# Attention, a product layer and a routed layer in one kernel: items of chunk 2 leave chunk 0's last two steps, and three hand-written orders are changed

## The chip, the cores and the metric

The kernel runs on one core of one Trainium2 chip. The metric is the device time of one execution in microseconds (us), as the median of several runs. A core has five engines that each run their own queue of instructions in order: TensorE (PE, with PEld for its weight loads), VectorE (DVE), ScalarE (ACT), GpSimd (POOL) and SyncE (SP, which issues most DMAs here). They meet at semaphores. Matrix products are written to PSUM, which is used here in named banks, everything else lives in SBUF.

## The reference

Three layers follow each other over N = 2304 tokens of 512 features (4 batches of 576 tokens, 8 heads of 64):

```python
scores = where(mask, q @ k^T / sqrt(64) + bias, -1e9)      # causal, window 128
x = softmax(scores) @ v                                     # (2304, 512)
x = ((x @ w_a) * (x @ w_b)) @ w_out                         # d_ff = 1536
logits = x @ w_gate + modality_bias[modality_id]            # 8 experts
e = argmax(logits); gate = softmax(logits)[e]
out = gate * (relu(x @ w1[e]) @ w2[e])                      # d_ff = 1024, one expert per token
```

All of it is float32. Products that need the full precision are made from two parts of each operand, a high part that is rounded for TensorE's fast format and the rest, as three matmuls (high times high, high times rest, rest times high). In the arrays the weights `w_a`, `w_b` and `w_out` are 64-bit floats; the kernel turns them into 32-bit ones with integer operations on VectorE (`f64_ops`, L422 and L426, three operations for each piece).

## The kernel before

**Tiles and chunks.** The 18 tiles of 128 tokens are cut into seven chunks of `CH = [3,2,2,3,3,3,2]` tiles. For each chunk the middle layer runs in 12 steps j, one for each 128 of the 1536 inner features. A step multiplies the chunk's x by the column pieces j of `w_a` and `w_b` (`mm_ab`, L513, 12 matmuls each, into banks `ab0` and `ab1`), copies the first product to SBUF (`asb`, ACT), multiplies the second by it (`gf`, DVE), splits `gf` into high part and rest (`g`: ACT, then DVE) and adds the product of the step before with its piece of `w_out` into the bank of each token tile (`mm_out`, L526 in chunk 0, L530 later).

**Attention as items.** Attention is cut into 72 items, one for each chunk, pair of heads and token tile; items 0 to 11 are chunk 0's, 12 to 19 chunk 1's, 20 to 27 chunk 2's. While a chunk's middle layer runs, its steps also carry the items of the chunk that comes next. The table `goal` says up to which item the scores are made by the end of each step. An item passes through three steps. In the first its scores are made (`ps_s`, PE; L254 for chunk 1's items, L258 for later ones), masked and reduced (DVE L266, L272) and exponentiated (ACT L282). In the next step the sums are inverted (DVE L288, L290), the exponentials scaled (ACT L301), transposed (`ps_p`, PE L310), copied as `pc` (ACT L323, DVE L324) and masked into `pt` by two selects (POOL L326, L328). In the third `a_pv` multiplies `pt` by V (`ps_o`, PE L378), and `pv_out` copies it out of its bank (`u`, ACT L387), moves one part across partitions (`z`, a DMA) and adds the parts into `xf` (POOL L392, and L393 once `z` has landed). When a chunk's items are done, `x_split` makes `xr` from `xf` (ACT L412, DVE L413), which the next chunk's L513 multiplies. Each pair of heads of chunk 2 or later is prepared once: `kk` (ACT L173, DVE L177), `qq` (ACT L183, DVE L188) and `vv` (ACT L197, DVE L201). `new_preps` starts them two steps ahead by `goal`; their DVE half is put off to the next step (`late_rests`).

**What chunk 0 does besides.** In chunk 0 the steps (`step0`) also convert weights. VectorE makes 32-bit floats of the next step's pair of pieces (`f64f`, jobs `w`) and of a piece of `w_out` (`f64o`, `wo_jobs`); ScalarE makes the high part of the pair (`wab`, L454, the "high parts"), VectorE the rest (L457). `mm_out` of chunk 0 uses `f64o` straight. In the last step (j = 11) two pieces of `w_out` are converted. In chunk 1 each step splits one piece of `w_out` into high part and rest (`wo_split`: ACT L497, DVE L498).

**Routing.** When a chunk's middle layer is done its token tiles are copied out (L634), and the router of the third layer runs for them during the next chunk. For chunks 0 and 1 that is `route` and `route_fin`: transposes (L542), then logits (L550) and arithmetic on VectorE (L557 to L576), then the rank of each token within its expert, two short matmuls (L585, L586) and five small VectorE operations (L587 to L592). One token tile takes three steps; the state in `tr` says where it stands.

**What sets the order.** The order of PE, ACT and DVE is the order in which the code is written, by hand. That of POOL and SP is left to a scheduler. `step0` writes out the order of VectorE's jobs as a string of letters: `w` an operation on the output weights, `l` the same for the last piece, `i` an inversion, `a` an operation on the pair's weights.

## Time and profile before

| what | value |
|---|---|
| median of 3 runs | 818.93 us (818.31 to 819.97) |
| the profiled execution, whole | 818.71 us |
| its span, first to last instruction | 816.9 us |
| chunk 0's steps | about 34 to 136 us |
| chunk 1's steps | about 136 to 204 us |
| chunk 2's steps | about 204 to 273 us |

The page gives PE 97% of the span as busy, DVE 67%, ACT 56% and POOL 29%. Matmuls are pipelined in the records, so what a reader looks for on PE is not its busy share but the places where a row of its timeline has an idle time in brackets, with the engine, tile and line that ended it. Between rows the distance from start to start is the time that a piece of work takes from the engine. The mean granted clock of TensorE is 0.995 of full speed over the span, and 1.00 in the three stretches of the table.

### The profile page before, as it was taken

To read this page: it belongs to the slowest core of one execution; us is meant where nothing else is said; L and a number is where in the kernel's file an instruction comes from. 1 tells how busy PE (TensorE), PEld (TensorE's weight loads), DVE (VectorE), ACT (ScalarE), POOL (GpSimd) and SP (SyncE) were. 2 spreads that over 40 slices of the span, in tenths; PEclk is the share of its full clock that TensorE was granted. 3 is DMA by queue.
4 is the path that set the end of the run, shared out by engine and by line. 5 is a ranking of instruction groups with operands and counts; after the bars stand their busy time and mean duration, and the time that the engine had idled before them with its cause. 6 is when DMAs were issued, how large, how long until landed. Compare 5 with 4: busy or idle time off the path is not lost.

```text
span 816.9 us, 14394 instructions
## 1 busy us (share of the span) xinstructions
PE 796.3 (97%) x4686; PEld 720.6 (88%) x4686; DVE 547.7 (67%) x1581; ACT 461.3 (56%) x1171; POOL 236.6 (29%) x365
## 2 busy tenths in 40 slices
PE   9999989999999999999999999999999999999994
PEld 7877767898899999999999999999988898989893
DVE  7899997777666766768776776468676544447410
ACT  6865447877678766666667643223436454457420
POOL 5332361443243333333333331120233030303101
PEclk9999999999999999999999999999999999999997
DMA  8977546777656875554556544566539464629201
GB/s 242 367 252 263 172 134 178 216 227 232 176 161 175 208 192 160 143 170 132 164 145 155 137 131 127 147 193 211 191 102 318 162 207 117 221 93 325 103 14 41
DMA packets 78629, 145.13 MB, mean 178 GB/s; under 512 B 14095, under 2 KB 41903, under 8 KB 78544
## 3 DMA queue, kind: packets, MB, share of 16 engines
q1 hardware_dynamic: 74992, 134.39, 54.7%
q0 software_dynamic: 3552, 9.73, 3.2%
q8 instruction: 39, 0.64, 0.3%
q14 instruction: 46, 0.38, 0.2%
HBM read 118.16 MB, written 22.12 MB: 172 GB/s over the span
## 4 chain that ended last, share of the span: by engine, by line
PE 62%; issue 14%; DVE 11%; ACT 7%; POOL 2%; DMA 2%; SPq 0%; POOLq 0%; ACTq 0%; DVEq 0%
PE ps_ab L513 29%; PE acc L530 12%; PE ps_h L1316 5%; PE ps_y L1299 4%; PE ps_o L378 2%; PE ps_s L258 2%; DVE f64f L426 2%; PE acc L526 2%; ACT p L282 2%; PE ps_p L310 1%; POOL out L1306 1%; PE ps_s L254 1%; DVE f64o L426 1%; POOL xg L940 1%; DMA wr<-in_moe_w 1%
## 5 line engine op out<-in xcount | busy, mean ns | idle before, releaser
L513 PE MATMUL ps_ab<-xr,wab 128*128 128x384 f32 (+1 forms) x2016 | 325.3, 316 | 0.9 <-DVE xr L413 0.7
L513 PEld LDWEIGHTS ps_ab<-xr,wab 128*128 128x128 f32 x2016 | 306.7, 188 | 11.8 <-issue 2.6
L530 PE MATMUL acc<-wo,g 128*128 128x512 f32 x540 | 135.4, 393 | 0.0
L326 POOL TENSOR_SCALAR_AFFINE_SELECT pt<-pc 128x512 fp32r<-128x512 f32 (+1 forms) x72 | 48.2, 669 | 257.1 <-DVE pc L324 232.6
L530 PEld LDWEIGHTS acc<-wo,g 128*128 128x128 f32 x540 | 96.9, 188 | 16.9
L1316 PE MATMUL ps_h<-xT,w1s 128*128 128x384 f32 x576 | 104.4, 337 | 0.0
L1299 PE MATMUL ps_y<-w2s,h 128*128 128x512 f32 x432 | 103.2, 393 | 0.0
L1316 PEld LDWEIGHTS ps_h<-xT,w1s 128*128 128x128 f32 x576 | 99.9, 188 | 0.9
L1299 PEld LDWEIGHTS ps_y<-w2s,h 128*128 128x128 f32 x432 | 79.8, 188 | 15.6
L282 ACT ACTIVATE p<-p,mx 128x128 f32<-128x128 f32 x144 | 56.8, 396 | 35.3 <-DVE mx L272 35.2
L613 DVE CUSTOM_DVE_ANT_0 junk<-x,wgt 128x512 f32<-128x512 f32 x88 | 62.3, 708 | 2.0
L1306 POOL DMA_INDIRECT out<-y,idx x18 | 20.4, 1134 | 133.1 <-ACT y L1305 131.9
L387 ACT COPY u<-ps_o 64x384 f32<-64x384 f32 x120 | 56.9, 474 | 2.0 <-PE ps_o L378 0.6
L1148 ACT CAST g<-gf 128x384 fp32r<-128x384 f32 (+1 forms) x60 | 28.2, 471 | 50.7 <-DVE gf L1146 50.3
L301 ACT ACTIVATE p<-p,mx 128x128 f32<-128x128 f32 x120 | 41.8, 395 | 26.7 <-DVE mx L290 26.5
L1149 DVE TENSOR_TENSOR g<-gf,g 128x384 fp32r<-128x384 f32 (+1 forms) x60 | 30.3, 505 | 38.1 <-ACT g L1148 38.1
L1146 DVE TENSOR_TENSOR gf<-ps_ab,asb 128x384 f32<-128x384 f32 (+1 forms) x60 | 30.1, 502 | 32.2 <-PE ps_ab L513 25.0
L900 DVE TENSOR_TENSOR w2s<-wr,w2s 128x1024 fp32r<-128x1024 f32 x24 | 29.2, 1224 | 32.9 <-ACT w2s L899 32.8
L900 DVE TENSOR_TENSOR w1s<-wr,w1s 128x1024 fp32r<-128x1024 f32 x28 | 34.3, 1224 | 20.9 <-ACT w1s L899 20.7
L328 POOL TENSOR_SCALAR_AFFINE_SELECT pt<-pc 128x512 fp32r<-128x512 f32 (+1 forms) x72 | 48.2, 669 | 0.0
L1319 ACT ACTIVATE h<-ps_h 128x384 fp32r<-128x384 f32 x48 | 23.6, 491 | 40.0 <-PE ps_h L1316 40.0
L392 POOL TENSOR_TENSOR xf<-u 128x128 f32<-128x128 f32 x60 | 33.5, 558 | 43.3 <-ACT u L387 43.3
(218 smaller groups left out, 1200.5 us busy)
## 6 DMA issues: line engine op xcount, KB each, us to landing
wo<-wo_d SPq DMA_DIRECT2D x60, 512.0 KB, 3.9
wr<-in_moe_w SPq DMA_DIRECT2D x56, 512.0 KB, 4.4
wgt<-in_wgt SPq DMA_DIRECT2D x32, 256.0 KB, 3.6
wraw<-in_moe_w_a SPq DMA_DIRECT2D x12, 512.0 KB, 5.7
wraw<-in_moe_w_b SPq DMA_DIRECT2D x12, 512.0 KB, 6.2
wor<-in_moe_w_out SPq DMA_DIRECT2D x12, 512.0 KB, 3.8
wo_d<-wo SPq DMA_DIRECT2D x12, 512.0 KB, 3.5
kr<-in_k SPq DMA_DIRECT2D x24, 256.0 KB, 4.1
```

The costliest lines, as they stand in the source:

```text
L282: nc.scalar.activation(out=it.p[:, h, :], in_=it.p[:, h, :], func=AF.Exp, bias=it.mx[:, 2 + h:3 + h], scale=-1.0, accum_out=it.mx[:, 4 + h ...
L301: nc.scalar.activation(out=it.p[:, h, :], in_=it.p[:, h, :], func=AF.Copy, scale=it.mx[:, 6 + h:7 + h])
L326: nc.gpsimd.affine_select(out=it.pt[:, :, 0], in_=pc, pattern=pat + [[-1, P]], base=0, channel_multiplier=1, compare_op=ALU.is_gt, fill=0.0)
L328: mark["pt"] = nc.gpsimd.affine_select(out=it.pt[:, :, 1], in_=pc, pattern=pat + [[1, P]], base=0, channel_multiplier=-1, compare_op=ALU.i ...
L387: nc.scalar.copy(out=u[o:o + 64], in_=it.po[o:o + 64, 1 - h:4 - h])
L392: nc.gpsimd.tensor_tensor(out=xf, in0=u[:, 0], in1=u[:, 2], op=ALU.add)
L513: nc.tensor.matmul(ps[:, :n], lhsT=w[:, m, r, kk * P:(kk + 1) * P], rhs=xr[:, s, kk, :n], start=(idx == 0), stop=(idx == len(terms) - 1))
L530: nc.tensor.matmul(acc[c, t], lhsT=g[:, r, t * P:(t + 1) * P], rhs=w[:, s, :], start=(j == 0 and idx == 0), stop=(j == NJ - 1 and idx == 2))
L613: nc.vector.tensor_tensor_reduce(out=junk, in0=x2[:, 0:DM], in1=wgt[e % len(wgt)], scale=1.0, scalar=0.0, op0=ALU.mult, op1=ALU.add, accum ...
L900: nc.vector.tensor_tensor(out=dst[:, 1], in0=srcw, in1=dst[:, 0], op=ALU.subtract)
L1299: nc.tensor.matmul(pss[t], lhsT=h[:, r, f, t * P:(t + 1) * P], rhs=W2[f // 2][:, s_, f % 2, :], start=(f == 0 and i == 0), stop=(f == 7 an ...
L1316: nc.tensor.matmul(ps, lhsT=W1[f // 2][:, r, kk, (f % 2) * P:(f % 2 + 1) * P], rhs=xT[:, s_, kk, :], start=(kk == 0 and i == 0), stop=(kk ...
```

## The change

There are five edits.

- `goal`: in chunk 0 the steps 10 and 11 make no scores any more; before, they made those of items 20 and 21, chunk 2's first two. Chunk 1's twelve steps take 11 items in place of 9. The preparations of the pairs move with the items.
- `step0`, from j = 2 on: `pv_out` stands ahead of the high parts of the pair's weights (before: at the end of the step's copies). The adds of `z` follow in the same step.
- `step0`: in a step with an inversion the third operation on the output weights goes ahead of the first one on the pair's.
- `step0`: `late_rests` stands ahead of the last operation on the pair's weights (before: behind the high parts).
- `route_fin`, for tiles of chunks 0 and 1: it pauses behind the two rank matmuls, and `step` lets the five VectorE operations run in the next step, behind the inversions and the late rests. Before, they followed the matmuls in VectorE's queue at the end of a step.

```diff
--- before.py
+++ after.py
@@ -584,6 +584,8 @@
             pr = ps_acc.tile([P, E], F32, tag=f"acc{t}", name="ps_r")
         nc.tensor.matmul(pr, lhsT=tri, rhs=oh, start=True, stop=False)
         nc.tensor.matmul(pr, lhsT=ones, rhs=osum, start=False, stop=True)
+        if late and t is not None:
+            yield
         nc.vector.tensor_tensor(out=osum, in0=osum, in1=oh, op=ALU.add)
         ra = rt.tile([P, E], F32, tag="ra", name="ra")
         nc.vector.tensor_tensor(out=ra, in0=pr, in1=ereg, op=ALU.add)
@@ -982,8 +984,8 @@
 
     n1_ = n0 + NP * CH[1]
 
-    goal = [n0 + 2 + max(0, min((3 * j + 2) // 4, n1_ - n0 - 2)) for j in range(NJ - 2)] + [n1_ + 1, n1_ + 2]
-    s0 = n1_ + 2
+    goal = [n0 + 2 + max(0, min((3 * j + 2) // 4, n1_ - n0 - 2)) for j in range(NJ)]
+    s0 = n1_
     for c in range(1, NC - 1):
         m = min(NP * C0[c + 2] + AHEAD, len(items)) - s0
         w = NJ if c < NC - 2 else NJ - 3
@@ -1042,9 +1044,12 @@
         if j > 1:
             lists = {"w": wo_jobs(j - 1), "i": [f for g in sc for f in score_invs(live[g])], "a": w[1:3],
                      "l": wo_jobs(j) if last else []}
-            for k in "wliwliawla" if sc else "wlawlwla":
+            for k in ("wliwliwla" if sc else "wlawlwl"):
                 if lists[k]:
                     lists[k].pop(0)()
+            late_rests()
+            if lists["a"]:
+                lists["a"].pop(0)()
             assert not any(lists.values())
         psa = mm_ab(0, j, 0) if j > 1 else ab_ps[0]
         asb = m1.tile([P, MT * P], F32, tag="asb", bufs=1, name="asb")
@@ -1081,17 +1086,17 @@
                 f()
             late_rests()
         else:
+
+            for it in its:
+                pv_out(it)
             for f in w[3::2]:
                 f()
-            late_rests()
             f_gf()
             for f in w[4::2]:
                 f()
             scores()
             pts()
             z_add()
-            for it in its:
-                pv_out(it)
         for g in new:
             score_red(live[g])
         for g in new:
@@ -1121,7 +1126,10 @@
         for g in sc:
             score_nrm(live[g])
         late_rests()
-        if tr and tr[0][0] == 1:
+        if tr and tr[0][0] == 5:
+
+            next(tr.pop(0)[1], None)
+        elif tr and tr[0][0] == 1:
             next(tr[0][1])
             tr[0][0] = 2
         asb = m1.tile([P, MT * P], F32, tag="asb", bufs=1, name="asb")
@@ -1175,10 +1183,10 @@
         if pend is not None:
             mm_out(*pend)
         if tr and tr[0][0] in (0, 2, 4):
-            next(tr[0][1], None)
+            next(tr[0][1])
             tr[0][0] += 1
             if tr[0][0] == 5:
-                next(tr.pop(0)[1], None)
+                next(tr[0][1])
         cur["s"] = goal[k]
         return (c, j, gt, wo_t[j]), new, sc
```

Three places show what becomes of it. The first is ScalarE in chunk 0, the middle of step 3. `asb` is the copy of the first product, `p` the scaling, `wab` the high parts, `pc` the copy of the transposed weights, `u` the copy out of the bank of `ps_o`. Before:

```order
L1051 COPY asb<-ps_ab_952 128x384
L301 ACTIVATE p<-p,mx 128x128 x2
L454 CAST wab_989<-f64f 128x512 x2
L323 CAST pc<-ps_p 128x2x128
L387 COPY u<-ps_o 64x384 x2
```

Now:

```order
L1056 COPY asb<-ps_ab_953 128x384
L301 ACTIVATE p<-p,mx 128x128 x2
L387 COPY u<-ps_o 64x384 x2
L454 CAST wab_997<-f64f 128x512 x2
L323 CAST pc<-ps_p 128x2x128
```

The copies `u` now stand ahead of the high parts.

The second is PE in chunk 0 from the item's product in step 10 on; `acc` are `mm_out`'s banks. Before:

```order
L378 MATMUL ps_o<-pt,vv 128x2x128 x4
L258 MATMUL ps_s<-kk,qq 128x256 x4
L526 MATMUL acc_831<-f64o,gf 128x512
L526 MATMUL acc_832<-f64o,gf 128x512
L526 MATMUL acc_833<-f64o,gf 128x512
L513 MATMUL ps_ab_1607<-xr_131,wab_1552 128x384 x12
L513 MATMUL ps_ab_1624<-xr_131,wab_1552 128x384 x12
L258 MATMUL ps_s<-kk,qq 128x256 x4
L310 MATMUL ps_p<-ident,p 128x128 x2
```

Now:

```order
L378 MATMUL ps_o<-pt,vv 128x2x128 x4
L526 MATMUL acc_831<-f64o,gf 128x512
L526 MATMUL acc_832<-f64o,gf 128x512
L526 MATMUL acc_833<-f64o,gf 128x512
L513 MATMUL ps_ab_1578<-xr_131,wab_1553 128x384 x12
L513 MATMUL ps_ab_1593<-xr_131,wab_1553 128x384 x12
L526 MATMUL acc_831<-f64o,gf 128x512
```

The two `ps_s` and the `ps_p` have left; they stand in chunk 1's steps 0 and 1 now.

The third is VectorE in chunk 1, around the first rank. `osum`, `ra`, `po_all` are the rank's operations, `mx` the inversions, `wo` the rest of the output weights, `kk` and `vv` rests of a pair. Before (step 2's end and step 3):

```order
L569 TENSOR_SCALAR sc<-sc 128x1
L570 RECIPROCAL x_1685<-sc 128x1
L587 TENSOR_TENSOR osum<-osum,oh 128x8
L589 TENSOR_TENSOR ra<-ps_r,ereg 128x8
L590 TENSOR_TENSOR ra<-ra,oh 128x8
L591 TENSOR_REDUCE sc<-ra 128x1
L592 CAST po_all<-sc 128x1
L288 TENSOR_SCALAR mx<-mx 128x2
L290 RECIPROCAL mx<-mx 128x2
L498 TENSOR_TENSOR wo<-wo 128x512
L201 TENSOR_TENSOR vv<-vr_2_1109,vv 128x3x128
L1146 TENSOR_TENSOR gf<-ps_ab_2021,asb 128x256
```

Now (the same place):

```order
L570 RECIPROCAL x_1630<-sc 128x1
L288 TENSOR_SCALAR mx<-mx 128x2
L290 RECIPROCAL mx<-mx 128x2
L498 TENSOR_TENSOR wo<-wo 128x512
L177 TENSOR_TENSOR kk<-kr_2_1105,kk 128x2x384
L201 TENSOR_TENSOR vv<-vr_1_847,vv 128x3x128
L589 TENSOR_TENSOR osum<-osum,oh 128x8
L591 TENSOR_TENSOR ra<-ps_r,ereg 128x8
L592 TENSOR_TENSOR ra<-ra,oh 128x8
L593 TENSOR_REDUCE sc<-ra 128x1
L594 CAST po_all<-sc 128x1
L1154 TENSOR_TENSOR gf<-ps_ab_1930,asb 128x256
```

The rank's five operations stand behind the inversions, behind `wo` and directly ahead of `gf`, and this step now also carries the rest `kk` of a pair.

## Rows read from the trace of the kernel before

**Rows 1.** Busy time of each engine, chunk 0's steps and chunk 1's: PE, PEld, DVE, ACT, POOL.
```profile
34.00:136.00 102.00, 97.41 (x458) 76.53 (x457) 95.39 (x195) 54.66 (x147) 36.86 (x45) 1.00 0.64 214
136.00:204.00 68.00, 67.46 (x498) 62.63 (x498) 49.40 (x170) 54.52 (x153) 26.24 (x42) 1.00 0.71 217
```

**Rows 2.** Timeline of PE, chunk 0: start, length, line, tiles, count, [idle before, releaser].
```profile
63.20 2.84 PE L526 MATMUL acc<-f64o,gf 128*128 128x512 f32 x6 [0.58 <-DVE f64o L426]
...
96.05 2.84 PE L526 MATMUL acc<-f64o,gf 128*128 128x512 f32 x6 [0.61 <-DVE f64o L426]
...
103.70 0.39 PE L378 MATMUL ps_o<-pt,vv 128*128 128x256 f32 x1 [0.64 <-POOL pt L326]
...
105.27 0.62 PE L378 MATMUL ps_o<-pt,vv 128*128 128x256 f32 x3 [1.19 <-POOL pt L328]
...
120.29 0.70 PE L378 MATMUL ps_o<-pt,vv 128*128 128x256 f32 x4
...
122.13 0.93 PE L258 MATMUL ps_s<-kk,qq 128*128 128x256 f32 x4 [1.14 <-DVE qq L188]
```

**Rows 3.** Timeline of POOL, the two selects of chunk 0's step 9.
```profile
116.17 3.10 POOL L326 TENSOR_SCALAR_AFFINE_SELECT pt<-pc 128x512 fp32r<-128x512 f32 x1 [5.76 <-DVE pc L324]
119.23 1.09 POOL L328 TENSOR_SCALAR_AFFINE_SELECT pt<-pc 128x512 fp32r<-128x512 f32 x1
```

**Rows 4.** Timeline of DVE, chunk 1, steps 0 to 3.
```profile
139.00 0.42 DVE L1146 TENSOR_TENSOR gf<-ps_ab,asb 128x256 f32<-128x256 f32 x1
...
143.40 0.95 DVE L177 TENSOR_TENSOR kk<-kr,kk 128x768 fp32r<-128x768 f32 x1
...
144.73 0.42 DVE L1146 TENSOR_TENSOR gf<-ps_ab,asb 128x256 f32<-128x256 f32 x1
...
149.31 0.99 DVE L188 SCALAR_TENSOR_TENSOR qq<-qr,qscale,qq 64x256 fp32r<-64x256 f32 x2
...
150.34 0.17 DVE L557 TENSOR_TENSOR lg<-ps_l,bm 128x8 f32<-128x8 f32 x1
...
151.35 0.42 DVE L1146 TENSOR_TENSOR gf<-ps_ab,asb 128x256 f32<-128x256 f32 x1
...
154.06 0.26 DVE L587 TENSOR_TENSOR osum<-osum,oh 128x8 bf16<-128x8 bf16 x1
...
155.05 0.16 DVE L288 TENSOR_SCALAR mx<-mx 128x2 f32<-128x2 f32 x1
```

**Rows 5.** Timeline of PE, chunk 1.
```profile
138.29 0.63 PE L378 MATMUL ps_o<-pt,vv 128*128 128x256 f32 x4
...
149.28 0.64 PE L378 MATMUL ps_o<-pt,vv 128*128 128x256 f32 x4
...
155.95 0.62 PE L310 MATMUL ps_p<-ident,p 128*128 128x128 f32 x2 [0.24 <-ACT p L301]
...
169.31 3.12 PE L513 MATMUL ps_ab<-xr,wab 128*128 128x256 f32 x24
...
172.27 0.65 PE L378 MATMUL ps_o<-pt,vv 128*128 128x256 f32 x4
...
172.88 0.71 PE L258 MATMUL ps_s<-kk,qq 128*128 128x256 f32 x4
...
173.44 1.55 PE L530 MATMUL acc<-wo,g 128*128 128x512 f32 x6
...
174.83 0.60 PE L542 MATMUL ps_x<-ident,x 128*128 128x128 f32 x4
...
175.19 3.06 PE L513 MATMUL ps_ab<-xr,wab 128*128 128x256 f32 x24
...
180.17 0.95 PE L550 MATMUL ps_l<-wg,x2T 128*128 128x8 f32 x8
...
180.98 3.10 PE L513 MATMUL ps_ab<-xr,wab 128*128 128x256 f32 x24
```

**Rows 6.** Timeline of PE, chunk 2: its longest wait inside the chunk.
```profile
223.84 0.62 PE L310 MATMUL ps_p<-ident,p 128*128 128x128 f32 x2 [0.43 <-ACT p L301]
```

## The prediction

> **What bounds the kernel now.** I read first the busy time of each engine by stage [rows 1], then the timeline of TensorE (PE) for rows with an idle time in brackets [rows 2, 5, 6], and for each such row the timeline of the engine that ended the wait [rows 3, 4]. The reader is to see two different regimes. In chunk 0 PE is busy for 97.41 us of 102.00, and VectorE for 95.39: it converts the weights and hardly ever waits for anybody, so what PE waits for there is late because VectorE is full. PE's five waits from step 3 on are two on `f64o` (0.58 and 0.61), two on `pt` (0.64 and 1.19) and one on `qq` (1.14) [rows 2], 4.16 us in all. In chunk 1 PE is busy for 67.46 of 68.00 [rows 1], with one visible wait of 0.24 for the scaled `p` [rows 5]; VectorE is busy for 49.40 us only, but that share hides a chain. From one `gf` of VectorE to the next goes a round: `gf`, ScalarE's `g`, VectorE's rest of `g`, `pc`, the reduction of the scores, ScalarE's exponential, the inversion, the split of the output weights, the rests, `gf`. VectorE works through it in order and waits in it for ScalarE twice. That round is the second clock of chunk 1 beside PE's own.
>
> **Part 1: work that only moves.** Two `ps_s` at 0.56 (172.88 to 173.44) and one `ps_p`, which with a `ps_o` takes 0.61 (172.27 to 172.88) [rows 5], leave chunk 0 and are done in chunk 1. PE does them either way: nothing.
>
> **Part 2: chunk 0.** The wait of 1.14 goes, because the `ps_s` that waited isn't there any more, and the pair's `qq` rests, which were late, have left VectorE's queue for chunk 1; behind it `mm_out` finds its weights ready. What is left to gain ahead of it has a ceiling. In step 10 `ps_o` starts at 120.29 [rows 2], and the second select of its item ends at 119.23 + 1.09 = 120.32 [rows 3]: PE came just in time for `pt`. So whatever PE gains in steps 3 to 9, it waits here until `pt` is there, and `pt` hangs on `pc`, which VectorE reaches when it has done its queue. That queue gets shorter ahead of this point by one `kk` rest, 0.95 (the same shape as the row at 143.40 [rows 4]). Output weights ahead of the pair's bring `f64o` forward, not the sum of the work. So the two waits on `f64o` and the two on `pt`, 3.02 together, come back as waits at the next thing that VectorE makes, but for 0 to 0.95; I take 0.5. The copies `u` ahead of the high parts let POOL start its adds earlier, so that the selects no longer queue behind them: this decides the 0.64 and 1.19, and is under the same ceiling. The high parts now stand behind the copies `u`, which need `ps_o`; where `ps_o` is late, VectorE's rest of the pair's weights gets late with it. No row shows that; I bound it by nothing and by the longest lateness of a `ps_o`, 1.19 [rows 2], and take nothing, since `mm_out` behind it (2.84 long at 63.20) covers PE meanwhile. Chunk 0 then gains 1.14 + 0.5 = **1.6 us**; from 0.5 (VectorE slowed, the ceiling used up) to 4.2 (all five waits gone).
>
> What POOL's earlier adds do to VectorE no row here isolates. [rows 3] show one and the same kind of select at 3.10 and at 1.09 us, so the two engines hinder each other on this stretch. The Trainium skill, page "SBUF — State Buffer", section "Who interferes with whom", says that a VectorE instruction with two SBUF inputs contends with a GpSimd instruction that reads SBUF and that the one that issues first holds the shared pair. By that rule the adds, moved into the stretch of two-input conversions, are served at VectorE's cost or wait for it; chunk 0's gain would go towards 0.5 or below, which is the second rival. The 3.10 agrees with it.
>
> **Part 3: chunk 1.** Now nearly every step carries an item in all three stages, and pairs come every second step, so that rests of a pair fall into every step. The lengths of VectorE's pieces [rows 4]: a round is 144.73 − 139.00 = 5.73 with `kk` and `vv` rests of 144.73 − 143.40 = 1.33, so 4.40 without any. `qq` rests cost 150.34 − 149.31 = 1.03, the router's arithmetic 151.35 − 150.34 = 1.01. (4.40 + 1.03 + 1.01 = 6.44; the row pair 144.73 to 151.35 has 6.62.) The rank's five operations take 155.05 − 154.06 = 0.99. Before, they stood ahead of the inversion, where VectorE would have waited for the exponential anyway; now they stand behind it and count in full. In return the scaling of `p` is earlier by most of a microsecond in those steps.
>
> The rounds that end in `gf` of steps 2 to 9, by the new order: `qq` + router 6.44; `kk`, `vv` + rank 4.40 + 1.33 + 0.99 = 6.72; `qq` 5.43; `kk`, `vv` + router 6.74; `qq` + rank 6.42; `kk`, `vv` 5.73; `qq` + router 6.44; rank and one `vv` about 5.8. Sum 49.7. PE for the same eight [rows 5]: 2.96 (L513) + 0.61 + 0.56 + 1.39 (`acc`, 173.44 to 174.83) = 5.52, with transposes + 0.36 (174.83 to 175.19), with logits + 0.81 (180.17 to 180.98): 3 × 6.33 + 2 × 5.88 + 3 × 5.52 = 47.3. VectorE's round is the longer one by 2.4.
>
> PE feels this as soon as `gf` is about 2 us behind the end of L513, since `ps_p` of the next step waits for the scaling that ends the same round: `gf` at 151.35 was 2.07 behind (149.28), and the next `ps_p` waited 0.24 [rows 4, 5]. That slack is used up at once. Step 0 has neither `ps_o` nor `acc` now, so PE takes 0.56 + 0.36 + 2.96 = 3.9 to the end of step 1's L513 while the round takes 5.4 to 5.7; starting from 0.3 to 0.7 behind (139.00 against 138.29), `gf` of step 1 is 2 behind already. So PE pays: 2.4 for the eight rounds, 0.5 because step 1 has no `ps_o` (the table counted one), 0.3 at step 1 itself, 0.5 because chunk 3's first pair, prepared here, has a third more `kk` and `vv` (1.33 / 3 = 0.44) and more `qq`, 0.5 at chunk 2's `x_split`, which starts that much later; less the 0.24 that it paid before. **4.0 us lost**; from 2.5 (the larger pairs and the `x_split` hidden, a round 0.1 shorter) to 5 (ScalarE, busy for 54.52 of 68.00 already [rows 1], gets late as well).
>
> **Part 4: chunk 2.** Two of the moved ranks are there. The wait of 0.43 [rows 6] stands behind a rank and goes, and with no split of output weights its rounds are short enough to take the rank behind the inversion: 0.4 gained, 0 to 0.43.
>
> **Sum.** The profiled execution took 818.71 in all, 1.8 more than its span of 816.9 and 0.22 less than the median of 818.93. 818.71 − 1.6 + 4.0 − 0.4 = **820.7 us**, 0.2% above the median. About 0.2% (1.6 us) is what a measurement of this kernel can tell from no change, so the forecast lies at the edge of what can be told: a small loss.
>
> **Rivals.**
> - *Faster: the waits inside VectorE's round are slack.* If what the added items bring falls into the time that VectorE now waits for ScalarE, the mean round stays under PE's mean step of 5.9 (47.3 / 8) and chunk 1 costs nothing. For it: the rank did hide that way before, and 68.00 − 49.40 = 18.6 us of VectorE are idle. Against it: 6.62 was measured for a round of the kind that will be common. 818.71 − 1.6 − 0.4 = 816.7. The point is a mean round of 5.9, against 6.2 by the sum. Chance 0.14.
> - *Nothing gained in chunk 0: POOL's early adds take VectorE's time.* Then 1.14 at step 10 is offset by a queue that runs later, the gain is 0, and the time is 818.71 + 4.0 − 0.4 = 822.3. For it the 3.10 of [rows 3]; against it that the adds are few, one in a step. Chance 0.14.
> - *A wash.* The gain of chunk 0 is nearer its middle, 2.4, and chunk 1 costs its low end, 2.5: 818.71 − 2.4 + 2.5 − 0.4 = 818.4. Both bounds are close to what I took, so this is nearly as likely as the forecast. Chance 0.34.
>
> **How the numbers follow.** The forecast has 0.38, with 819.9 to 821.8 as its own range. Slower by over 0.2% (above 820.6) are all of the second rival and nine tenths of the forecast: 0.48. Within 0.2%: the wash and the rest of the forecast, 0.38. Faster by over 0.2% (below 817.3): the first rival, 0.14. The range leaves out most of the first rival, and the end of the second: 817.3 to 822.7.
>
> **What the profile of the changed kernel would show.** Right: no wait on `qq` at step 10, no waits on `f64o`, a wait on `pt` in step 10 in their place; chunk 0 shorter by about 2.9 in PE's timeline (1.6 and the moved work); in chunk 1 five or more waits of PE on `ps_p` or `ps_s` of 0.3 to 1.2 each, and `gf` 2 to 3.5 behind the end of L513 from step 1 to step 9; no wait of 0.43 in chunk 2. Wrong: PE in chunk 1 without brackets (the first rival), or `f64f` rows of VectorE in chunk 0 longer than before beside POOL's adds (the second).

## The result and the profile after

The changed kernel takes 823.75 us (median of 6 runs, 823.3 to 825.03) against 819.21 us for the kernel before in the same runs (818.31 to 820.73). The ratio is 1.0056, interval [1.0044, 1.0069]: slower, as forecast, but by 4.5 us where 2 were forecast, and outside the range. The profiled execution took 823.3 us, 4.6 above the profiled one of before, 2.6 above the predicted 820.7.

The first lines of its page (span, and busy time of each engine), then the line of busy times of the kernel before, then the two stretches of [rows 1] in the same columns after the change:

```profile
span 821.5 us, 14388 instructions
...
PE 801.3 (98%) x4686; PEld 721.0 (88%) x4686; DVE 548.1 (67%) x1581; ACT 461.9 (56%) x1171; POOL 229.3 (28%) x365
```
```profile
PE 796.3 (97%) x4686; PEld 720.6 (88%) x4686; DVE 547.7 (67%) x1581; ACT 461.3 (56%) x1171; POOL 236.6 (29%) x365
```
```profile
34.00:136.00 102.00, 98.14 (x462) 76.47 (x461) 92.63 (x177) 52.52 (x136) 31.86 (x43) 1.00 0.60 208
136.00:204.00 68.00, 66.29 (x477) 59.94 (x477) 49.48 (x182) 53.33 (x154) 22.64 (x40) 1.00 0.71 208
```

PE counts as busy for 5 us more than before, with the same instructions. So the busy share doesn't say where the time went; a row of PE can hold small gaps. What says it is the distance from start to start of the same product. Here are PE's rows of L513 that begin chunk 0, chunk 1, chunk 2's second step and chunk 3's second step, from the timeline, of before and then of after:

```profile
31.30 1.29 PE L513 MATMUL ps_ab<-xr,wab 128*128 128x384 f32 x6
...
135.08 3.38 PE L513 MATMUL ps_ab<-xr,wab 128*128 128x256 f32 x24
...
208.40 3.06 PE L513 MATMUL ps_ab<-xr,wab 128*128 128x256 f32 x24
...
278.30 4.32 PE L513 MATMUL ps_ab<-xr,wab 128*128 128x384 f32 x24
```
```profile
31.24 1.30 PE L513 MATMUL ps_ab<-xr,wab 128*128 128x384 f32 x6
...
133.43 3.38 PE L513 MATMUL ps_ab<-xr,wab 128*128 128x256 f32 x24
...
212.85 3.06 PE L513 MATMUL ps_ab<-xr,wab 128*128 128x256 f32 x24
...
283.51 4.32 PE L513 MATMUL ps_ab<-xr,wab 128*128 128x384 f32 x24
```

Between these marks lie what this text calls chunk 0, chunk 1 and chunk 2. The PE work that moves from the first to the second is counted in: two `ps_s` at 0.56 and a `ps_p` at 0.13 (172.75 to 172.88 in the trace of before), 1.25 us.

| stretch | before | after | difference | forecast |
|---|---|---|---|---|
| chunk 0 | 103.78 | 102.19 | -1.59 | -1.6 - 1.25 = -2.85 |
| chunk 1 | 73.32 | 79.42 | +6.10 | +4.0 + 1.25 = +5.25 |
| chunk 2 | 69.90 | 70.66 | +0.76 | -0.4 |

The sum is 5.27 against 2.0. All three terms are too favourable: by 1.26, 0.85 and 1.16. Some 0.6 us come back at the end, behind the last L513 at 580 us, since the spans differ by 4.6 only. From that row to the end the 17 profiles of this text take 235.9 to 237.0 us, without an edit there, so this is scatter.

PE's waits in chunk 0 are now these (the list of waits, in all, times, longest):

```profile
PE acc L526 <- DVE f64o L426: 1.9, 3, 1.1
PE ps_ab L513 <- ACT wab L454: 0.8, 2, 0.6
PE ps_p L310 <- ACT p L301: 0.8, 2, 0.4
PE ps_o L378 <- POOL pt L328: 0.4, 1, 0.4
```

The wait on `qq` and most of those on `pt` [rows 2] have gone. Waits on weights have come in their place: those on `f64o` were to go and grew from 1.2 us to 1.9, those on `wab` are new. In step 10 and in chunk 1 the timeline of PE shows:

```profile
120.14 0.63 PE L378 MATMUL ps_o<-pt,vv 128*128 128x256 f32 x4
121.82 2.84 PE L526 MATMUL acc<-f64o,gf 128*128 128x512 f32 x6 [1.05 <-DVE f64o L426]
...
153.75 0.62 PE L310 MATMUL ps_p<-ident,p 128*128 128x128 f32 x2 [0.48 <-ACT p L301]
...
160.22 0.62 PE L310 MATMUL ps_p<-ident,p 128*128 128x128 f32 x2 [0.20 <-ACT p L301]
161.16 0.93 PE L258 MATMUL ps_s<-kk,qq 128*128 128x256 f32 x4 [0.32 <-DVE qq L188]
```

From one `gf` of VectorE to the next, step 1 to step 9 of chunk 1 (timeline of DVE; [rows 4] have those of before), after shows eight rounds in 194.20 - 142.32 = 51.88 us, 6.5 each. Before, the same eight took 189.87 - 144.73 = 45.14 us, 5.6 each. The last row here is before's:

```profile
142.32 0.42 DVE L1154 TENSOR_TENSOR gf<-ps_ab,asb 128x256 f32<-128x256 f32 x1
...
194.20 0.42 DVE L1154 TENSOR_TENSOR gf<-ps_ab,asb 128x256 f32<-128x256 f32 x1
```
```profile
189.87 0.41 DVE L1146 TENSOR_TENSOR gf<-ps_ab,asb 128x256 f32<-128x256 f32 x1
```

In steps 1 to 9 `gf` of after starts 1.5 to 3.4 us behind the PE row that follows L513, where 2 to 3.5 were forecast.

### The profile page after: what moved, and what is told of

It is laid out like the page before. It is cut to its first block, busy times and chain, and to the rows that moved or that the text cites. A ratio compares the mean times of both kernels' runs of the same rounds, so it can differ in the third digit from the quotient of the medians.

```text
span 821.5 us, 14388 instructions
## 1 busy us (share of the span) xinstructions
PE 801.3 (98%) x4686; PEld 721.0 (88%) x4686; DVE 548.1 (67%) x1581; ACT 461.9 (56%) x1171; POOL 229.3 (28%) x365
## 4 chain that ended last, share of the span: by engine, by line
PE 56%; DVE 15%; issue 15%; ACT 9%; POOL 2%; DMA 1%; SPq 0%; POOLq 0%; ACTq 0%; DVEq 0%
PE ps_ab L513 25%; PE acc L530 11%; PE ps_h L1324 6%; PE ps_y L1307 4%; DVE f64f L426 3%; ACT p L282 2%; PE ps_s L258 2%; PE ps_o L378 2%; PE acc L526 1%; DVE f64o L426 1%; POOL out L1314 1%; DVE wab L457 1%; PE ps_s L254 1%; PE ps_p L310 1%; DVE ps_s L266 1%
## 5 line engine op out<-in xcount | busy, mean ns | idle before, releaser
L513 PE MATMUL ps_ab<-xr,wab 128*128 128x384 f32 (+1 forms) x2016 | 324.4, 316 | 1.8 <-ACT wab L454 0.8
L513 PEld LDWEIGHTS ps_ab<-xr,wab 128*128 128x128 f32 x2016 | 306.6, 188 | 14.1 <-ACT wab L454 5.2
L326 POOL TENSOR_SCALAR_AFFINE_SELECT pt<-pc 128x512 fp32r<-128x512 f32 (+1 forms) x72 | 46.1, 640 | 272.5 <-DVE pc L324 247.8
L328 POOL TENSOR_SCALAR_AFFINE_SELECT pt<-pc 128x512 fp32r<-128x512 f32 (+1 forms) x72 | 45.2, 628 | 0.0
L1328 DVE SCALAR_TENSOR_TENSOR h<-ps_h,h 128x384 fp32r<-128x384 f32 x48 | 26.3, 553 | 24.3 <-ACT h L1327 24.3
```

What stands on the lines that cost most here:

```text
L326: nc.gpsimd.affine_select(out=it.pt[:, :, 0], in_=pc, pattern=pat + [[-1, P]], base=0, channel_multiplier=1, compare_op=ALU.is_gt, fill=0.0)
L328: mark["pt"] = nc.gpsimd.affine_select(out=it.pt[:, :, 1], in_=pc, pattern=pat + [[1, P]], base=0, channel_multiplier=-1, compare_op=ALU.i ...
L513: nc.tensor.matmul(ps[:, :n], lhsT=w[:, m, r, kk * P:(kk + 1) * P], rhs=xr[:, s, kk, :n], start=(idx == 0), stop=(idx == len(terms) - 1))
```

## The experiments

**How to read them.** Each kernel's profile gives the three stretches, which repeat to about 0.1 us in chunks 0 and 1, and to 0.4 in chunk 2, from one kernel to the next where nothing was edited. One thing disturbs them. In some executions TensorE's granted clock falls for some 3.4 us, once, at a place where PE has just waited. The windows of the kernel `a_goal` below show it (us, PE's busy time, granted clock):

```profile
104.00:106.00 2.00, 0.81 (x6) 1.00 0.33 124
106.00:108.00 2.00, 2.00 (x6) 0.54 0.08 16
108.00:110.00 2.00, 2.00 (x4) 0.61 0.08 16
110.00:112.00 2.00, 2.00 (x10) 1.00 0.05 4
```

PE had waited 0.63 and 1.19 us for `pt` from 103.0 to 105.2, the same waits as in [rows 2]; then it ran at 1.2 GHz in place of 2.4 for 3.4 us (twice the 2 x 0.46 + 2 x 0.39 that is missing). The same kernel without the fall (`a_goal_2`) has that step at 10.43 us, this one at 12.13: 1.7 us. The kernel before seems to have the fall in some executions and not in others: of its 27 runs beside the first four kernels, 15 lie at 817.65 to 819.12 us (14 of them with a mean granted clock of 0.995 or more) and 12 at 819.85 to 821.55 (all at 0.994 or less). That these are the two kinds is inferred, since only one of its executions was profiled. The mean clock alone doesn't tell them apart: each profile also has the lower level in its last 6 to 9 us, after shows 0.994 without a fall, and in later batches of before some runs at 0.994 take 818.3 to 818.8 us. The profiled execution of before has no fall in these chunks, and neither has that of after.

So chunk 0 is compared with 1.7 taken off where the table has a star. `b_ranks`, whose edit leaves chunk 0 alone, agrees: with the fall it is 1.63 longer than before. For the falls in step 10 (`c_step0`, `f_wo`, `g_late`, `q_mm8`) the 1.7 is an estimate from these two. In chunk 1 the same fall costs less: the two starred kernels there, 79.46 and 79.40, are only 0.7 to 0.8 longer than `a_goal_2` with the same work in chunk 1. That fits a chunk in which PE has waits to fill. The ratios are of medians, which hold the falls.

| kernel | edit | ratio, interval | chunk 0 | chunk 1 | chunk 2 |
|---|---|---|---|---|---|
| before | | 1 | 103.78 | 73.32 | 69.90 |
| after | all | 1.0056 [1.0044, 1.0069] | 102.19 | 79.42 | 70.66 |
| a_goal | items moved | 1.0034 [1.0016, 1.0053] | 102.63* | 78.67 | 70.10 |
| a_goal_2 | the same again | 1.0031 [1.0016, 1.0045] | 100.91 | 78.71 | 70.44 |
| b_ranks | ranks | 1.0015 [1.0003, 1.0026] | 105.41* | 74.40 | 70.44 |
| c_step0 | three orders | 1.0018 [1.0007, 1.0030] | 106.87* | 73.38 | 69.90 |
| d_noranks | after less ranks | 1.0034 [1.0019, 1.0048] | 102.13 | 78.68 | 70.22 |
| e_pvout | PV copies early | 1.0004 [0.9995, 1.0013] | 103.53 | 73.29 | 69.80 |
| f_wo | output weights early | 1.0038 [1.0025, 1.0051] | 107.06* | 73.38 | 69.98 |
| g_late | late rests early | 1.0015 [1.0006, 1.0024] | 106.20* | 73.30 | 70.16 |
| o_goal_wo | items, output weights | 1.0034 [1.0024, 1.0044] | 101.76 | 79.40* | 70.54 |
| o_goal_late | items, late rests | 1.0032 [1.0022, 1.0041] | 101.72 | 79.46* | 70.20 |
| j_wopool | after, `wo` rests on POOL | 1.0075 [1.0062, 1.0088] | 102.18 | 81.29 | 70.39 |
| k_nowo | after, no `wo` rests | 0.9995 [0.9986, 1.0005] | 102.21 | 75.34 | 70.75 |
| p_mmfirst | before, `mm_out` early | 0.9986 [0.9977, 0.9996] | 102.68 | 74.07 | 70.11 |
| q_mm8 | the same, step 8 only | 1.0012 [1.0001, 1.0024] | 105.53* | 73.31 | 70.03 |
| t_mmpv | both early | 1.0038 [1.0027, 1.0049] | 106.88 | 74.02 | 70.05 |

**The parts one by one.** First the four that split the change into items, ranks and orders.

*Items moved, alone* (`a_goal`):
```diff
-    goal = [...for j in range(NJ - 2)] + [n1_ + 1, n1_ + 2]
-    s0 = n1_ + 2
+    goal = [...for j in range(NJ)]
+    s0 = n1_
```


> The kernel before with one part of the change alone: the last two steps of chunk 0 take no items of chunk 2, all of them go to chunk 1. Orders of VectorE and the ranks stand as before. Theory 1 (the loss is VectorE's round in chunk 1, which became longer than a step of TensorE because of the added rests): this part alone brings nearly the whole loss. Chunk 1 (first L513 of chunk 1 to chunk 2's second step) was 73.32 us before and 79.42 after; here 77.5 to 79, a little less than after since the ranks still stand where VectorE waits anyway. Time 2.5 to 4.5 us above before. Theory 2 (the loss comes from the new order in chunk 0 and 1, copies ahead of the high parts and POOL's adds that take VectorE's time): this part alone costs 0 to 1 us, or gains up to 1. Theory 3 (the loss is the ranks behind the inversions): 0 to 1 as well.

Measured: 822.12 us, 1.0034 [1.0016, 1.0053]. Chunk 1 is 78.67, the 77.5 to 79 of theory 1: 5.35 longer than before, 4.1 of it more than moved work. That is most of what chunk 1 loses, and it is there without any new order.

*Ranks alone* (`b_ranks`; the change's edits to `route_fin` and `step`, nothing else):
```diff
+        if late and t is not None:
+            yield
         nc.vector.tensor_tensor(out=osum, in0=osum, in1=oh, op=ALU.add)
```


> The kernel before with the ranks' operations behind the inversions, alone. Theory 1: chunk 1 has room in VectorE's round before the items are added, so 0 to 0.8 us lost there; the wait of 0.43 in chunk 2 goes, but the rank's 0.99 us of VectorE now counts in that chunk's rounds, which is 0 to 0.6 lost in the step of the second rank (6.11 us against 5.51 in the changed kernel). Together -0.4 to +0.8. Theory 3 (the ranks are the loss): +2 or more.

Measured: 820.28 us, 1.0015 [1.0003, 1.0026]. Of chunk 0's 105.41, 1.7 are the fall of the clock. Chunk 1 is 1.08 longer and chunk 2 0.54, not shorter: a loss of 1.6 where at most 0.8 was expected. The ranks are not free even in the kernel before.

*The three orders alone* (`c_step0`):
```diff
-            for k in "wliwliawla" if sc else "wlawlwla":
+            for k in ("wliwliwla" if sc else "wlawlwl"):
...
+            late_rests()
+            if lists["a"]:
+                lists["a"].pop(0)()
...
+            for it in its:
+                pv_out(it)
             for f in w[3::2]:
                 f()
-            late_rests()
```


> The kernel before with the new orders of VectorE alone: copies of the PV banks ahead of the high parts, output weights ahead of the pair's, rests of items behind them. Theory 1: -1.0 to +0.5 us; chunk 0 has VectorE full, an order doesn't change the sum of its work. Theory 2 (POOL's earlier adds and the order cost VectorE time): +1.5 or more, and it shows in chunk 0, whose two-input f64f conversions get longer.

Measured: 820.74 us, 1.0018 [1.0007, 1.0030], more than the 0.5 us that theory 1 allowed. Chunk 0 without the fall is 105.2, 1.4 longer; chunks 1 and 2 are as before. It is the place that theory 2 names. Its cause, longer conversions, is there in part: VectorE's integer conversions (L422, L426) take 59.2 us here and 58.3 before. But with the items moved they take 59.3 us with the old orders (`a_goal_2`) and 59.3 with the new (after), and there the orders cost 1.28 all the same (below). So the orders cost time without longer conversions too.

*After with the ranks back* (`d_noranks`):
```diff
-        if late and t is not None:
-            yield
...
-        if tr and tr[0][0] == 5:
-            next(tr.pop(0)[1], None)
-        elif tr and tr[0][0] == 1:
+        if tr and tr[0][0] == 1:
...
-                next(tr[0][1])
+                next(tr.pop(0)[1], None)
```


> The changed kernel with the ranks back ahead of the inversions. Theory 1: chunk 1 is bound by VectorE's round, so each of the about 2 ranks in it gives back up to 0.99 us less what p's scaling loses: 0.4 to 1.2 us below the changed kernel in chunk 1 (78.2 to 79.0 for 79.42), the wait of 0.43 in chunk 2 comes back and its step with the second rank is 5.5 again. Time 3 to 4.2 us above before (the changed kernel: 4.5). Theory 3: less than 1 above before.

Measured: 822.06 us, 1.0034 [1.0019, 1.0048], 3.2 above before, in the range of theory 1. In chunk 1 it takes back 0.74, in chunk 2 0.44. With `b_ranks` this gives the ranks 1.2 to 1.6 us.

**Is it VectorE's round?** Two kernels take the rests of the output weights in chunk 1 from VectorE.

*Onto GpSimd* (`j_wopool`):
```diff
-        nc.vector.tensor_tensor(out=w[:, 1], in0=f, in1=w[:, 0], op=ALU.subtract)
+        nc.gpsimd.tensor_tensor(out=w[:, 1], in0=f, in1=w[:, 0], op=ALU.subtract)
```


> The changed kernel with the rests of the output weights in chunk 1 made by GpSimd (1.41 us for this shape) and not by VectorE (0.69 us, and 4.3 us in all of waiting for ScalarE's half). Theory 1 (VectorE's round is what chunk 1 loses to): each round of VectorE gets 0.7 to 1.1 shorter, 5.2 to 5.5 on average, below a step of TensorE; chunk 1 to chunk 2's second step falls from 79.4 to 74.8 to 76, the time by 3 to 4.5 us, to 819.3 to 820.8. Rival S (ScalarE, busy for 53 of 68 us, is the late one): chunk 1 stays within 0.7 of 79.4. Rival P (GpSimd's 1.41 stands ahead of its selects, and these come late instead): some of it, 77 to 79, with waits for pt.

Measured: 824.86 us, 1.0075 [1.0062, 1.0088]; chunk 1 is 81.29, longer, where each theory said equal or shorter. The timelines of DVE and then POOL at two of these rests:

```profile
160.22 1.90 DVE L188 SCALAR_TENSOR_TENSOR qq<-qr,qscale,qq 64x256 fp32r<-64x256 f32 x2
...
166.99 1.65 DVE L201 TENSOR_TENSOR vv<-vr,vv 128x384 fp32r<-128x384 f32 x1
```
```profile
160.37 1.46 POOL L498 TENSOR_TENSOR wo<-wo 128x512 fp32r<-128x512 f32 x1
...
166.28 1.95 POOL L498 TENSOR_TENSOR wo<-wo 128x512 fp32r<-128x512 f32 x1
```

A pair of `qq` rests takes 1.90 us beside POOL's rest and 0.99 [rows 4] without it, a `vv` rest 1.65 against 0.55. VectorE got rid of 0.69 and paid 0.9 to 1.1. So its round became longer and chunk 1 with it, which speaks for the round, but not cleanly. The Trainium skill, page "SBUF — State Buffer", section "Who interferes with whom", says that a VectorE instruction with two SBUF inputs contends with a GpSimd instruction that reads SBUF; these rows agree.

*Left out* (`k_nowo`; no engine does it):
```diff
-        nc.vector.tensor_tensor(out=w[:, 1], in0=f, in1=w[:, 0], op=ALU.subtract)
```


> The changed kernel without VectorE's rests of the output weights in chunk 1 (0.69 us in each step, and 4.3 us of waiting in all for ScalarE's half); the second half keeps the unsplit weights, so the sum is another one. No engine gets this work. Theory 1 (VectorE's round binds chunk 1): chunk 1 to chunk 2's second step falls from 79.4 to 74.5 to 76 us, near the 73.3 + 1.25 that TensorE needs, and the waits on p and qq there go; time 3.5 to 5 us below the changed kernel. Rival S (ScalarE's chain of exponential, g, casts is what is late): 78.5 to 79.4.

Measured: 819.33 us, 0.9995 [0.9986, 1.0005]; chunk 1 is 75.34, 4.08 shorter than in after, inside the 74.5 to 76 of theory 1. VectorE's eight rounds take 48.29 us, 0.45 less each. ScalarE's work is the same in both. What is left of PE's waits in chunk 1:

```profile
PE ps_p L310 <- ACT p L301: 0.8, 2, 0.6
PE ps_ab L512 <- DVE xr L413: 0.4, 1, 0.4
```

Taking an operation of 0.69 us out of each of VectorE's rounds gives PE 4.08 of the 4.85 us back that chunk 1 lost beyond the moved work. The round is what chunk 1 loses to, and rival S, by which ScalarE's load alone would hold it, falls. What ScalarE's share of the round is worth stays open: in after's chunk 1 VectorE waits 8.3 us for `g` and 7.3 us for the exponential, and no run made these shorter.

**What the orders cost in chunk 0.** Three singles on the kernel before:

*PV copies ahead of the high parts* (`e_pvout`):
```diff
+            for it in its:
+                pv_out(it)
             for f in w[3::2]:
                 f()
             late_rests()
...
             z_add()
-            for it in its:
-                pv_out(it)
```


> The kernel before with one of the three new orders of chunk 0 alone: the PV banks are copied out ahead of the pair's high parts. The three orders together made chunk 0 (from its first to chunk 1's first product with the pair's weights) 106.9 us for 103.8, of which 1.7 are a stretch of 3.4 us at the clock's lower level, so 1.4 longer by themselves. Theory U (ScalarE's copies u hold back its high parts, and VectorE's rests of the pair's weights wait for them: 3.3 us of such waits in 11 places for 2.3 in 6): the whole 1.4 comes with this order, though the two waits for pt of 0.6 and 1.2 go: chunk 0 at 104.5 to 105.5 us, waits of VectorE on the high parts at 3.0 or more. Rival W (the output weights ahead of the pair's make the pair's late): here a gain of 1 to 1.8 us, since the waits for pt go and nothing else changes.

Measured: 819.47 us, 1.0004 [0.9995, 1.0013]; chunk 0 is 103.53, 0.25 shorter, and VectorE waits for the high parts as before, 2.3 in 6 places. Theory U falls for this kernel, and rival W's gain of 1 to 1.8 isn't there either: the waits for `pt` shrink from 2.2 to 1.3 us, but those for `f64o` grow from 1.2 to 1.5 and one for `p` of 0.2 is new. The conversions take 58.1 us, so POOL's earlier adds alone don't lengthen them.

*Output weights ahead of the pair's* (`f_wo`):
```diff
-            for k in "wliwliawla" if sc else "wlawlwla":
+            for k in ("wliwliwlaa" if sc else "wlawlwla"):
```


> The kernel before with the output weights' conversions of chunk 0 ahead of the pair's last jobs, alone. Theory U: within 0.5 us of before, waits of VectorE on the high parts as before (2.3). Rival W: chunk 0 1 to 1.5 us longer, and TensorE waits for the pair's weights (wab), which it did not before.

Measured: 821.77 us, 1.0038 [1.0025, 1.0051]; chunk 0 without the fall is 105.4, 1.6 longer. The size is just above rival W's 1 to 1.5, the place isn't the one it names: PE waits 3.6 us for `qq` in step 10 (1.14 before), not for the pair's weights. The conversions take 59.4 us here, 1.1 more than before.

*Late rests ahead of the last operation on the pair's weights* (`g_late`):
```diff
-            for k in "wliwliawla" if sc else "wlawlwla":
+            for k in ("wliwliawl" if sc else "wlawlwl"):
                 if lists[k]:
                     lists[k].pop(0)()
+            late_rests()
+            if lists["a"]:
+                lists["a"].pop(0)()
...
-            late_rests()
             f_gf()
```


> The kernel before with the items' late rests moved from behind the high parts to a place ahead of the step's products, alone. Theory U: within 0.5 us of before. Rival L (rests that are not due yet delay the weights, by up to 0.95 for a kk): chunk 0 0.5 to 1.4 us longer, in the two or three steps with such a rest.

Measured: 820.41 us, 1.0015 [1.0006, 1.0024]; chunk 0 without the fall is 104.5, 0.7 longer, and VectorE's waits for the high parts are 3.3 in 11 places: rival L. The timelines of DVE in step 8 show how, of before and then of `g_late`:

```profile
95.92 1.22 DVE L426 SCALAR_TENSOR_TENSOR f64f<-wraw,f64f 128x1024 uint32<-128x1024 uint32 x1
97.05 0.55 DVE L201 TENSOR_TENSOR vv<-vr,vv 128x384 fp32r<-128x384 f32 x1
97.52 0.55 DVE L1058 TENSOR_TENSOR gf<-ps_ab,asb 128x384 f32<-128x384 f32 x1
97.99 1.28 DVE L457 TENSOR_TENSOR wab<-f64f,wab 128x512 fp32r<-128x512 f32 x2
```
```profile
96.30 0.55 DVE L201 TENSOR_TENSOR vv<-vr,vv 128x384 fp32r<-128x384 f32 x1
96.77 1.22 DVE L426 SCALAR_TENSOR_TENSOR f64f<-wraw,f64f 128x1024 uint32<-128x1024 uint32 x1
97.91 0.55 DVE L1061 TENSOR_TENSOR gf<-ps_ab,asb 128x384 f32<-128x384 f32 x1
98.67 1.29 DVE L457 TENSOR_TENSOR wab<-f64f,wab 128x512 fp32r<-128x512 f32 x2 [0.22 <-ACT wab L454]
```

Before, the `vv` rest filled the time in which ScalarE cast the high part that L426 had just finished. Now it stands ahead of L426: the high part is later by its length, and VectorE waits where it had cover. In after, which has the same order, this step's L513 waited 0.60 us for `wab`.

*On top of the moved items* (`a_goal`'s edit with `g_late`'s is `o_goal_late`, with `f_wo`'s `o_goal_wo`; `a_goal_2`, the items alone once more, is their base):


> The kernel before with the items moved (as in the run of that part alone) and the late rests ahead of the step's products, without the other two orders. With the three orders chunk 0 of the moved items is 102.1 us; without them 102.6, of which 1.7 are at the clock's lower level, so the orders together cost 1.2. Theory L (the late rests' place carries it: VectorE's waits for ScalarE's high parts rise to 3.3 us in 11 places, as with this order alone on the kernel before): 1 to 1.4 here, chunk 0 at 101.9 to 102.3, or 1.7 above where the clock falls. Rival W (the output weights): 0 to 0.4, 100.9 to 101.3.

> The kernel before with the items moved and the output weights ahead of the pair's, without the other two orders. Theory L: chunk 0 at 100.5 to 101.3 (1.7 more where the clock falls). Rival W: 101.9 to 102.5 (1.7 more where the clock falls), and a wait of TensorE for the pair's weights or of VectorE for TensorE.

> The kernel with the items moved and nothing else, once more, for an execution in which the clock doesn't fall. If the fall is all that separates it, chunk 0 is 100.9 us (102.6 less 1.7), 1.2 below the three orders' 102.1, and the time about 820.6. If VectorE or ScalarE would have been the next late anyway (the gain of an unbroken clock is waited for later), chunk 0 is 101.5 to 102.2 and the orders cost less than 0.7.

Measured: `a_goal_2` has chunk 0 at 100.91, the 100.9 that were expected of the items alone; 821.31 us, 1.0031 [1.0016, 1.0045]. So the three orders add 102.19 - 100.91 = 1.28. `o_goal_late` (822.21 us) has 101.72 and `o_goal_wo` (822.26 us) 101.76: 0.8 to 0.9 each, between what theory L and rival W said of them. Neither carries it alone, and the two don't add up. The fall of the clock came in chunk 1 in both.

From L513 to L513 the three orders do what they were made for and pay for it elsewhere: from `a_goal_2` to after, step 8, where the waits for `pt` were, falls from 10.43 to 8.48 us, 1.95 less, and the steps 3, 4, 7, 9 and 10 get 0.41, 0.37, 0.80, 0.57 and 1.00 longer.

**A version that gains.** PE's waits of [rows 2] in steps 8 and 10 can be filled with `mm_out` of the step before, whose operands are there (`p_mmfirst`, on the kernel before):
```diff
+        first = j in (8, 10)
+        if first:
+            mm_out(*pend, wo_t[j - 1])
         for it in its:
             a_pv(it)
...
-        mm_out(*pend, wo_t[j - 1])
+        if not first:
+            mm_out(*pend, wo_t[j - 1])
```


> The kernel before, with the output product of the step before (mm_out) ahead of the attention products in steps 8 and 10 of chunk 0, where TensorE waited 0.64 + 1.19 us for pt and 1.14 us for qq; mm_out's weights and gf are ready there. If these waits are TensorE's own loss, and if the clock's fall that some executions show right behind them comes from them: chunk 0 (103.8 us) 1.5 to 2.9 shorter, no stretch at the clock's lower level, time 816 to 817.5, 1.5 to 2.5 us below the median of before. Rival (the ceiling: VectorE is full, so what TensorE gains there it waits for the weights of the next steps): chunk 0 0 to 0.7 shorter, and only the clock's part of 0 to 1.7 is gained.

Measured: 818.18 us against 819.20, 0.9986 [0.9977, 0.9996]: a small gain in the median over both kernels, but not the 816 to 817.5 that were expected. Chunk 0 is 1.1 shorter, between forecast and rival. PE now waits 2.5 us for `f64o` in four places (the ceiling is real), and chunk 1 gives 0.75 back, chunk 2 another 0.2. So the three stretches together gain 0.1, and its lowest time, 817.78, is next to before's 817.87. What the median gains is at the upper end: its runs end at 819.29 where the kernel before reaches 821.17, and its profile has no fall of the clock. That it never has one is not shown.

*Step 8 only* (`q_mm8`):
```diff
-        first = j in (8, 10)
+        first = j in (8,)
```


> The kernel before with the output product ahead of the attention products in step 8 of chunk 0 alone (TensorE waited 0.64 + 1.19 us for pt there), not in step 10. If the waits in step 8 precede the fall of the clock, no fall at 106 to 110 us; the wait of 1.1 for qq in step 10 is still there and may have one of its own behind it at 124 us. Chunk 0 0.3 to 1 us below 103.8 without a fall.

Measured: 820.48 us, 1.0012 [1.0001, 1.0024]. Chunk 0 without the fall is 103.8, no shorter than before, where 0.3 to 1 were expected. There is no fall at 106 to 110 us; there is one behind the wait for `qq` in step 10. The same windows as above:

```profile
120.00:122.00 2.00, 0.62 (x3) 1.00 0.36 135
122.00:124.00 2.00, 1.71 (x5) 0.55 0.14 23
124.00:126.00 2.00, 2.00 (x4) 0.59 0.30 88
```

The mean clock of all its ten runs is 0.994 or less, the profiled one's too, which fits a fall in each but doesn't show it. In the one execution that was profiled, with the first wait filled, the fall stood behind the next.

*Both* (`t_mmpv`: the edit of `p_mmfirst` and that of `e_pvout`):


> The kernel before with the output product ahead in steps 8 and 10 (that alone gave 818.18 us and chunk 0 at 102.7), and the PV banks copied out ahead of the pair's high parts (alone: chunk 0 at 103.5). If each has a gain of its own, chunk 0 at 102.3 to 102.5, time 817.8 to 818.1. If VectorE's conversions are the ceiling of both, no change from 818.18.

Measured: 822.01 us, 1.0038 [1.0027, 1.0049]; chunk 0 is 106.88, 4.2 longer than in `p_mmfirst`. ScalarE and VectorE in step 8 (timelines of ACT, then DVE):

```profile
107.06 0.97 ACT L387 COPY u<-ps_o 64x384 f32<-64x384 f32 x2 [6.31 <-PE ps_o L378]
108.06 1.14 ACT L454 CAST wab<-f64f 128x512 fp32r<-128x512 f32 x2
```
```profile
108.71 1.29 DVE L457 TENSOR_TENSOR wab<-f64f,wab 128x512 fp32r<-128x512 f32 x2 [3.45 <-ACT wab L454]
```

With `ps_o` late, the copies of it hold ScalarE's high parts behind them, and VectorE stands for 3.45 us. Neither of the two expectations had this. It is theory U's mechanism, and it costs nothing where `ps_o` is in time, as in `e_pvout`, and much where it isn't.

## Why the prediction was wrong, and where it was right

**What bounds the kernel**: right. In chunk 0 whatever an order took out of step 8 came back in other steps, at `f64o`, `qq` and `wab`, which VectorE makes or feeds, and chunk 1 hangs on VectorE's round.

**Part 1**, moved work at nothing: nothing speaks against it. `a_goal_2` shortens chunk 0 by 2.87, which is 1.25 of moved work and 1.62 more.

**Part 2**, chunk 0 gains 1.6: the moved items gave 1.62, and the orders, which were taken at nothing, cost 1.28. So 0.34 was gained, just below the range's 0.5. That 1.62 meets 1.6 is in part luck. Step 10 of `a_goal_2` (timeline of PE) has `ps_o` and `mm_out` next to each other:

```profile
120.00 0.63 PE L378 MATMUL ps_o<-pt,vv 128*128 128x256 f32 x4
120.47 2.74 PE L526 MATMUL acc<-f64o,gf 128*128 128x512 f32 x6
```

Before, the same way took from 120.29 to 122.90, 2.61 us, of which `ps_o` needs 0.47 and `ps_s` 0.56. So the wait on `qq` was worth 1.58, not the 1.14 of its bracket [rows 2], and this is nearly the whole 1.62. The 0.5 for the shorter queue didn't come: the waits on `f64o`, 1.2 us, and on `pt`, 2.2, stand in `a_goal_2` as before.

The step that failed is the price of the orders. Output weights ahead of the pair's were to bring `f64o` forward, "not the sum of the work", and the place of the late rests has no term in the sum at all. With the items moved the sum did stay, 59.3 us of conversions with either set of orders. But what covers ScalarE's casts did not stay: the waits of VectorE for the high parts rose from 2.5 us in 7 places (`a_goal_2`) to 3.3 in 11, as with the late rests' place alone. The waits that were to come back "but for 0 to 0.95" came back with more: step 8 gained 1.95 and the other steps lost 3.2. The late rests alone cost 0.81 on the moved items, and the rows of `g_late` show how in one step. The output weights alone cost 0.85 while those waits rose by 0.2 only; what carries this, and how the two make 1.28 together, stays open.

The ceiling held, but it was hung on the wrong row: not `pt` was late in step 10, but `f64o` (1.05 at 121.82), and waits on `f64o` were to go. The lateness of `ps_o`, bounded by 0 to 1.19 and taken at nothing, was right for the order of before by `e_pvout`; `t_mmpv`, in which `ps_o` stands behind `mm_out`, shows that it can cost more where PE's order is another.

**Part 3**, chunk 1 loses 4.0: the right mechanism, and 6.10 - 1.25 = 4.85 measured, within the 2.5 to 5. Its terms were mis-sized in both directions. The eight rounds were added up to 49.7 and measured 51.88, seven of them 0.09 to 0.48 longer than their sums (6.53, 7.18, 5.53, 7.10, 6.90, 6.01, 6.82, 5.81). Against the 47.3 that the same part counted for PE this is 4.6 of the 4.85, so the small terms (1.6 net) can have been worth only a few tenths. By part: the items 4.1 (`a_goal`), the ranks 0.74 more (after against `d_noranks`), where the sum had counted 2 of them in full, 1.98. The sign was seen, but smaller: five bracketed waits for `p` and `qq` of 0.20 to 0.48 us, where 0.3 to 1.2 were named. With chunk 2's `x_split` (0.42) the brackets of the stretch hold 2.0 us only; the rest sits inside the recorded lengths of PE's rows, and only starts show it: `ps_p` at 160.22 is followed 0.94 us later by `ps_s`, before this took 0.13 (172.75 to 172.88).

**Part 4**, chunk 2 gains 0.4: wrong, it loses 0.76. The wait of 0.43 [rows 6] is gone and its step fell from 6.89 to 6.46, as said. What failed is "its rounds are short enough to take the rank behind the inversion". In the step with the second rank VectorE now does (timeline of DVE)

```profile
245.70 1.26 DVE L188 SCALAR_TENSOR_TENSOR qq<-qr,qscale,qq 64x384 fp32r<-64x384 f32 x2
246.99 0.16 DVE L589 TENSOR_TENSOR osum<-osum,oh 128x8 bf16<-128x8 bf16 x1
...
247.66 0.15 DVE L594 CAST po_all<-sc 128x1 int32<-128x1 f32 x1
247.74 0.42 DVE L1154 TENSOR_TENSOR gf<-ps_ab,asb 128x256 f32<-128x256 f32 x1
```

the larger `qq` rests of chunk 3 and the rank in a row, behind the inversion; before, the rank ended at 240.7 and the inversion followed it at once, so it filled VectorE's wait for the exponential (0.47 us in after, none before). The step takes 6.11 us, 5.85 in `d_noranks` and 5.51 before; the steps behind it lose 0.5 more together, at most 0.26 in one. By `d_noranks` the ranks are 0.44 of the 0.76, about what chunk 2 scatters, with 0.54 in `b_ranks` on the same side. The other 0.3 come with the items (0.2 in `a_goal`, 0.5 in `a_goal_2`), and their cause stays open.

**The rivals.** The first, that the waits in the round are slack, is refuted by `a_goal` and `k_nowo`; the mean round is 6.5, and its point was 5.9. The second, with 822.3, came nearest to the measured time. Its chunk 0, with no gain, is nearer the 0.34 than the forecast is, and its sign came: the `f64f` rows take 35.1 us in after and 34.1 before. But its mechanism isn't shown to be the cause: with POOL's early adds alone (`e_pvout`) these rows take 34.0, and what they gained in after against `a_goal_2` (34.2) the `f64o` rows gave back. The wash had both of its bounds wrong.

## What to carry to other kernels

An engine that is full can still be made later by an order that keeps its work: whatever stands between producing for another engine and reading its answer is cover, and moving it ahead can pay its length to the consumer and a wait to the engine (here a rest of 0.55 us and a wait of 0.22). Work that fills a wait inside a round costs nothing where it stands and its full length one place further on, so before moving it, add up the round that takes it with the largest tiles that it will meet, not those of the round that was read. And a loss is found by distances from start to start: here 4.85 us were lost in a stretch whose brackets hold 2.0, and a bracket of 1.14 was worth 1.58.

## What the runs showed of the hardware

TensorE's granted clock fell to 1.2 GHz for some 3.4 us behind single waits: after 0.63 and 1.19 us in a row of stops (`a_goal`, 106 to 110), after 1.1 with PE busy for 0.62 of 2.00 us (`q_mm8`, 122 to 126). In chunk 0 this cost 1.7 us (`a_goal` against `a_goal_2`), in chunk 1, where PE waits for VectorE anyway, 0.7 to 0.8 (`o_goal_late` and `o_goal_wo`). The very same waits at the same place had no fall in `a_goal_2` and in the profiled execution of before, so one profile of such a kernel doesn't give its median: for the kernel before the two groups of runs lie 2.3 us apart (medians 818.2 and 820.5), half of what the change cost. One fall accounts for 1.7 of these 2.3; the rest is not explained.
